# One copy moved ahead on ScalarE's list: the pad of the second chunk's keys

## The chip, the cores and the metric

The kernel runs on one core of a Trainium2 chip. The metric is the device time of one execution in microseconds (us). Five engines run their own instruction lists side by side and wait for each other by semaphores: TensorE (PE, matrix products into PSUM), VectorE (DVE), ScalarE (ACT), GpSimd (POOL) and SyncE (SP, which here only starts DMAs).

## What is computed

The input x has 2048 rows of 640 columns, in bf16. Its rows are normalised, and two branches are added to x:

```python
xn = _layernorm(x, axis=-1)
return x + _A_ref(xn, A_wqkv, A_wo) + _B_ref(xn, B_w1, B_b1, B_w2, B_b2)
```

Branch A is attention with 32 heads of 20 columns. Row s looks at 8 rows only, s, s-2, ..., s-14, so the keys and values of a row reach at most 14 rows back. Scores before row 0 are masked. Branch B is a two-layer perceptron, 640 to 1536 to 640, with gelu between.

## The kernel before

**Tiles.** The 2048 rows are cut into four chunks of 512 (the names use n = 0 to 3), each chunk into four blocks of 128 (j = 0 to 3). Activations stand transposed, features on the partitions and rows along the free dimension, in 5 tiles of 128 features. For each chunk `qT`, `kT` and `vT` hold queries, keys and values. `kT` and `vT` have 14 extra columns in front of each feature tile, the **pad**, which holds the last 14 rows of the chunk before, so that a window can reach back across the border.

**Stages of a chunk.** Mean and variance of the rows; normalised rows `xn` (line 262 on ScalarE), turned into `xnT` by a DMA on SP's queue (line 291, pieces `tc`); the projections q, k, v on TensorE (line 333, pieces `pj`, for the first chunk line 377, pieces `hj`), each copied from PSUM by ScalarE (line 397, pieces `pc`; line 392, pieces `hc`); the products q times k for the 8 window places on VectorE, one instruction per block (line 430, pieces `qk`); sums over feature tiles on VectorE (lines 465 and 471, pieces `pa`, `pb`) and over the columns of a head on TensorE (line 480, piece `lg`); the softmax (VectorE: maximum, difference, sum, lines 527 to 538; ScalarE: exponent, line 543, and reciprocal by Ln and Exp, lines 552 and 553, pieces `ri`); the weights spread over the partitions by DMAs (line 577, pieces `xe`); weights times values on VectorE (line 584, pieces `av`) and their sums. The perceptron runs beside this: line 614 (pieces `f1`) into PSUM, gelu on ScalarE (line 630, pieces `ge`), and line 696 (pieces `t`), which adds both branches up in PSUM.

**The order.** Nothing is scheduled by a program: the string `ORDER` names every piece of work once, the pieces are issued in that order, and each engine works through its own instructions in that order without overtaking. Waits come from the tiles: a reader waits for the writer, a writer waits for earlier readers of the same tile.

**PSUM banks.** The outputs of `pj`, `hj` and `f1` share one pool of four banks (`psA`). TensorE can begin such an output only when ScalarE has copied out one of those that hold the banks. ScalarE's place in its list therefore decides when TensorE goes on.

**Around the change.** The piece `pad11` is the pad of the keys (the second 1) of the second chunk (the first 1): one ScalarE copy of 5 times 14 columns per partition, line 404, out of the first chunk's keys into the second chunk's `kT`. The four products of the second chunk stand on VectorE in the order `qk11`, `qk13`, `qk12`, `qk10`. The products of blocks 1, 2 and 3 begin at column 128 or later of a feature tile, and only block 0 reads the pad columns. All four and the pad copy nevertheless touch the same tile, with the feature tiles of one between those of the other, and the built program orders them: a product that stands behind the pad copy in `ORDER` waits for it, and the pad copy waits for the products that stand ahead of it.

In `ORDER` of the kernel before, ScalarE has at this place: the last copies of the second chunk's q and k (the last one of k is `pc113`), a load of the activation table with exponents `ex0b` and `ex0a`, then `pc120`, `sq23`, `pc124`, `sq20` (squares for the third chunk's variance), `hc202`, `rs2` (lines 244 and 247), then `pad11`, `hc211`, `pc122`, `ri0b`, `ri0a`, `hc210`, a table load, `ge0_7`, `xn21`, `ge0_4`, `xn20`.

Of the kernel before, what the change touches and what calls it, by code (L numbers as in the profile page):

```python
# [43 lines left out]
xn10 hj012 hc110 tc10 hj011 pk xn11 hj111 hc012 tc11 hc010 qk00 hc011 hj112 hc111 f10_2 hc112 xn13 f10_0 xn12 tc13  # L44
qk02 f10_1 tc12 ge0_0 f10_5 ldx qk03 f10_11 ge0_5 f10_3 ge0_11 ge0_2 pj101 ge0_3 pa00 pj112 pc101 ge0_1 pj104 pc112
xp2 pa01 su20 pj110 xp0 pc104 ld2 su22 pj102 pc110 pb01 pj100 su21 hj201 su23 pc102 pb04 pj103 ng2 pc100 hc201 pj114
sq22 lg0 pc114 ldo pj111 cp0b cp0a sq21 mask pj113 m0b pc103 m0a pj124 pc111 mx0a pc113 mx0b t000 qk11 pj120 ex0b
hj202 ex0a hj210 pc120 sq23 ss0a hj211 pc124 ss0b sq20 pj122 qk13 hc202 rs2 f10_7 pad11 hc211 pc122 t040 ri0b f10_8
ri0a rc2 qk12 hc210 f10_4 f11_1 ge0_7 xn21 qk10 f11_3 ge0_4 tc21 xn20 pj121 ge1_3 tc20 t041 ge1_1 pa11 f11_9 ge0_8
xn23 hj212 pc121 tc23 t001 xn22 pa10 f10_6 hc212 tc22 ge1_9 f11_10 ge0_6 at0a at0b f10_9 ge1_10 pb11 xe01 su33 xe03  # L50
t002 xe00 ge0_9 pj123 pad21 su32 pb14 pj210 xe02 su31 pj203 xp1 pc210 su30 lg1 t042 pc203 av01 cp1b f10_10 ng3 f11_5
# [805 lines left out]
```

## Time and profile before

| what | value |
|---|---|
| median of 3 runs | 207.95 us (207.87 to 208.01) |
| the profiled execution | 207.52 us |
| its span, first to last instruction | 205.4 us |
| granted TensorE clock | 1.000 |
| busy: TensorE, VectorE, ScalarE, GpSimd | 200.2, 185.7, 129.0, 29.4 us |

The profile is of one execution. Times in its views are microseconds from the span's start. Each row of a timeline has the start, the length, the engine, the line in the kernel, what is written and read, and how many instructions are merged in the row; a bracket gives the idle time ahead of it and what ended that. Instructions of one engine can overlap by about a tenth of a microsecond in the records. TensorE's ends are modelled, so its starts are the better numbers.

### The profile page before, as it was taken

To read this page: it belongs to the slowest core of one execution; us is meant where nothing else is said; L and a number is where in the kernel's file an instruction comes from. 1 tells how busy PE (TensorE), PEld (TensorE's weight loads), DVE (VectorE), ACT (ScalarE), POOL (GpSimd) and SP (SyncE) were. 2 spreads that over 40 slices of the span, in tenths; PEclk is the share of its full clock that TensorE was granted. 3 is DMA by queue.
4 is the path that set the end of the run, shared out by engine and by line. 5 is a ranking of instruction groups with operands and counts; after the bars stand their busy time and mean duration, and the time that the engine had idled before them with its cause. 6 is when DMAs were issued, how large, how long until landed. Compare 5 with 4: busy or idle time off the path is not lost.

```text
span 205.4 us, 2870 instructions
## 1 busy us (share of the span) xinstructions
PE 200.2 (97%) x1100; PEld 105.1 (51%) x1100; DVE 185.7 (90%) x160; ACT 129.0 (63%) x237; POOL 29.4 (14%) x34
## 2 busy tenths in 40 slices
PE   8999999997899999999999999999999999999994
PEld 3998455573444555544445544444434454445552
DVE  2889998799995999999999998999979999998871
ACT  5679898887898799655284443996469942220100
POOL 2000000000000400022340040000022710253320
PEclk9999999999999999999999999999999999999999
DMA  6997499800428690759399181002845899893951
GB/s 207 391 396 191 104 378 337 305 0 0 67 64 218 178 191 4 199 117 142 79 161 121 19 97 15 3 0 39 191 51 93 146 102 161 134 107 57 101 89 64
DMA packets 38430, 27.31 MB, mean 133 GB/s; under 512 B 25106, under 2 KB 34578, under 8 KB 38418
## 3 DMA queue, kind: packets, MB, share of 16 engines
q1 hardware_dynamic: 28016, 20.39, 35.5%
q0 software_dynamic: 10080, 6.56, 28.0%
q10 hardware_dynamic: 322, 0.20, 0.3%
q8 instruction: 8, 0.13, 0.3%
q14 instruction: 4, 0.03, 0.0%
HBM read 10.49 MB, written 4.59 MB: 73 GB/s over the span
## 4 chain that ended last, share of the span: by engine, by line
PE 90%; DVE 5%; ACT 3%; issue 0%
PE T L696 26%; PE hps L614 23%; PE pps L333 21%; PE lo L652 5%; PE gps L377 5%; DVE prod L430 3%; PE idle L443 2%; PE both L652 2%; PE gps L346 1%; PE hi L652 1%; PE L L480 1%; DVE ax L529 1%; PE tp L279 1%; ACT L170 1%; ACT hT L630 1%; DVE ax L527 1%
## 5 line engine op out<-in xcount | busy, mean ns | idle before, releaser
L614 PE MATMUL hps<-xnT,w_sb 128*128 128x512 bf16 x240 | 56.3, 379 | 1.5 <-ACT vT L392 1.0
L430 DVE TENSOR_TENSOR prod<-qT,kT 128x5120 bf16<-128x5120 bf16 x16 | 44.6, 2821 | 1.4 <-ACT qT L397 1.0
L696 PE MATMUL T<-hT,w_sb 128*128 128x512 bf16 x180 | 44.6, 379 | 0.0
L614 PEld LDWEIGHTS <-w_sb 128*128 128x128 bf16 x240 | 23.4, 98 | 29.8 <-issue 2.3
L708 POOL DMA_DIRECT2D out_dram<-x_sb x15 | 20.8, 1593 | 67.1 <-DMA x_sb<-x_sb 67.1
L630 ACT ACTIVATE hT<-hps,bT 128x512 bf16<-128x512 f32 x36 | 23.8, 691 | 9.5 <-PE hps L614 9.1
L696 PEld LDWEIGHTS <-w_sb 128*128 128x128 bf16 x180 | 17.2, 98 | 20.9 <-issue 1.3
L584 DVE TENSOR_TENSOR prod<-vT,ax 128x5120 bf16<-128x5120 bf16 x8 | 22.4, 2821 | 3.6 <-PE L L480 3.6
L699 ACT ACTIVATE x_sb<-T,bT 128x512 bf16<-128x512 f32 x15 | 10.4, 693 | 21.6 <-PE T L696 19.2
L584 DVE TENSOR_TENSOR prod<-vT,x_sb 128x5120 bf16<-128x5120 bf16 x8 | 22.3, 2819 | 0.1
L595 POOL DMA_DIRECT2D prod<-prod x6 | 7.3, 1208 | 100.2 <-DVE prod L584 100.2
L170 ACT ACT_TABLE_LOAD x14 | 18.0, 1283 | 1.0 <-PEq L841 0.7
L471 DVE TENSOR_TENSOR prod<-prod 128x4096 bf16<-128x4096 bf16 x8 | 18.3, 2291 | 0.2
L333 PE MATMUL pps<-xnT,wv_sb 128*128 128x512 bf16 x75 | 18.3, 379 | 0.2
L696 PE MATMUL T<-oT,wo 128*128 128x512 bf16 x75 | 18.5, 379 | 0.0
L333 PE MATMUL pps<-xnT,wq_sb 128*128 128x512 bf16 x75 | 18.5, 379 | 0.0
L333 PE MATMUL pps<-xnT,wk_sb 128*128 128x512 bf16 x75 | 18.3, 379 | 0.0
L465 DVE TENSOR_TENSOR prod<-prod 128x4096 bf16<-128x4096 bf16 x8 | 18.1, 2287 | 0.1
L597 DVE TENSOR_TENSOR prod<-prod 128x2560 bf16<-128x2560 bf16 x10 | 14.6, 1484 | 0.0
L397 ACT CAST qT<-pps 128x512 bf16<-128x512 f32 x15 | 8.6, 583 | 7.2 <-PE pps L333 7.2
L333 PEld LDWEIGHTS <-wv_sb 128*128 128x128 bf16 x75 | 8.7, 117 | 7.8 <-issue 0.6
L333 PEld LDWEIGHTS <-wk_sb 128*128 128x128 bf16 x75 | 8.7, 118 | 7.7 <-issue 0.4
(96 smaller groups left out, 240.7 us busy)
## 6 DMA issues: line engine op xcount, KB each, us to landing
prod<-prod POOLq DMA_DIRECT2D x6, 640.0 KB, 6.5
ax<-attn SPq DMA_DIRECT2D x8, 256.0 KB, 4.3
x_sb<-attn SPq DMA_DIRECT2D x8, 256.0 KB, 4.2
w_sb<-in_B_w_dram SPq DMA_DIRECT2D x2, 960.0 KB, 11.5
out_dram<-x_sb SPq DMA_DIRECT2D x3, 640.0 KB, 5.0
w_sb<-in_B_w_dram SPq DMA_DIRECT2D x4, 480.0 KB, 6.9
out_dram<-x_sb POOLq DMA_DIRECT2D x15, 128.0 KB, 4.5
x_sb<-in_A_x_dram SPq DMA_DIRECT2D x2, 640.0 KB, 6.8
```

Of the source, the lines that this page charges most:

```text
L170: nc.scalar.preload_act_table_set(name)
L333: nc.tensor.matmul(ps[:], lhsT=wqkv_p[which][:, ti, to, :], rhs=xnT[:, ti, :], start=(ti == 0), stop=(ti == KT - 1),)
L430: nc.vector.tensor_tensor(out=prod[:, j], in0=q[:, :, at].unsqueeze(1).to_broadcast([P, W, KT, P]), in1=window(k, at), op=ALU.mult,)
L465: nc.vector.tensor_tensor(out=low, in0=low, in1=high, op=ALU.add)
L471: nc.vector.tensor_tensor(out=first, in0=first, in1=rows[:, :, t * P : (t + 1) * P], op=ALU.add)
L584: nc.vector.tensor_tensor(out=prod[:, j], in0=window(qkv_tile(n, 2), slice(j * P, (j + 1) * P)), in1=ax_view(n)[:, j, :, :].unsqueeze(2).t ...
L597: nc.vector.tensor_tensor(out=low, in0=low, in1=high, op=ALU.add)
L614: nc.tensor.matmul(ps[:], lhsT=w1_sb[:, ti, ft * P : (ft + 1) * P], rhs=tiles["xnT", n][:, ti, :], start=(ti == 0), stop=(ti == KT - 1),)
L630: nc.scalar.activation(hT, tiles["hps", n, ft][:], ACT.Gelu_apprx_tanh, bias=bT[:, ft : ft + 1], scale=1.0)
L652: nc.tensor.matmul(out_ps(bl, hi), lhsT=lhs, rhs=rhs[:, CH:D] if hi else rhs[:, 0:CH], start=pc == 0 and k == 0, stop=pc == 4 and k == len ...
L696: nc.tensor.matmul(ps[:], lhsT=lhs, rhs=rhs, start=pc == 0 and k == 0, stop=pc == 4 and k == len(srcs) - 1)
L708: nc.gpsimd.dma_start(dst, src, accum_op=ALU.add)
```

## The change

`pad11` is named 18 pieces earlier in `ORDER`: ahead of `qk11`, where it stood behind `qk13`, `rs2` and `f10_7`. No instruction is added or taken away, and no other piece changes its place against another.

```diff
-...mx0b t000 qk11 pj120 ex0b
-hj202 ex0a hj210 pc120 sq23 ss0a hj211 pc124 ss0b sq20 pj122 qk13 hc202 rs2 f10_7 pad11 hc211 pc122 t040 ri0b f10_8
+...mx0b t000 pad11 qk11 pj120
+ex0b hj202 ex0a hj210 pc120 sq23 ss0a hj211 pc124 ss0b sq20 pj122 qk13 hc202 rs2 f10_7 hc211 pc122 t040 ri0b f10_8
```

(The dots stand for the unchanged head of the first line.) On ScalarE the copy comes to stand between `pc113` and the table load. In the built program its single wait names `pc113`, the last write of `kT` ahead of it, where it named `qk13` before. `qk11` waits for the pad copy, where it waited for `pc113`. `qk12` has no wait left. The first Ln of `ri0b` (line 552) has a wait of its own for the last sum of `ss0b`, which the pad's wait covered before. The lists of the other engines are unchanged.

More of the change, by code (lines that the diff above doesn't have):

```diff
@@ L46 @@
 xp2 pa01 su20 pj110 xp0 pc104 ld2 su22 pj102 pc110 pb01 pj100 su21 hj201 su23 pc102 pb04 pj103 ng2 pc100 hc201 pj114
-sq22 lg0 pc114 ldo pj111 cp0b cp0a sq21 mask pj113 m0b pc103 m0a pj124 pc111 mx0a pc113 mx0b t000 qk11 pj120 ex0b
-hj202 ex0a hj210 pc120 sq23 ss0a hj211 pc124 ss0b sq20 pj122 qk13 hc202 rs2 f10_7 pad11 hc211 pc122 t040 ri0b f10_8
+sq22 lg0 pc114 ldo pj111 cp0b cp0a sq21 mask pj113 m0b pc103 m0a pj124 pc111 mx0a pc113 mx0b t000 pad11 qk11 pj120
+ex0b hj202 ex0a hj210 pc120 sq23 ss0a hj211 pc124 ss0b sq20 pj122 qk13 hc202 rs2 f10_7 hc211 pc122 t040 ri0b f10_8
 ri0a rc2 qk12 hc210 f10_4 f11_1 ge0_7 xn21 qk10 f11_3 ge0_4 tc21 xn20 pj121 ge1_3 tc20 t041 ge1_1 pa11 f11_9 ge0_8
```

## The prediction

> **What bounds the kernel now.** I read the page's first part, then busy time by stretches, the waits, and the rows of three engines from 39 to 65 us, where the moved copy stands.
>
> ```profile
> PE 200.2 (97%) x1100; PEld 105.1 (51%) x1100; DVE 185.7 (90%) x160; ACT 129.0 (63%) x237; POOL 29.4 (14%) x34
> ...
> 40.00:47.00 7.00, 6.96 (x44) 4.67 (x43) 6.86 (x8) 5.49 (x12) 0.00 (x0) 1.00 0.02 6
> 47.00:54.00 7.00, 5.37 (x25) 2.37 (x24) 6.75 (x5) 6.62 (x14) 0.00 (x0) 1.00 0.01 2
> 54.00:65.00 11.00, 11.00 (x60) 5.34 (x58) 8.69 (x6) 10.01 (x21) 0.00 (x0) 1.00 0.60 120
> 65.00:205.00 140.00, 137.64 (x701) 66.58 (x697) 130.18 (x91) 74.76 (x124) 27.90 (x22) 1.00 0.64 101
> ```
>
> The stretches give length, then busy time of PE, PEld, DVE, ACT and POOL, granted clock, DMA share, GB/s. TensorE is the bound: busy for all but 5.2 of 205.4 us. But 1.63 of those 5.2 lie between 47 and 54 us. Who is waited for there, in the waits between 36 and 66 us:
>
> ```profile
> DVE prod L584 <- PE L L480: 2.5, 1, 2.5
> ...
> ACT kT L404 <- DVE prod L430: 1.8, 1, 1.8
> PE hps L614 <- ACT vT L392: 1.0, 1, 1.0
> ...
> PE hps L614 <- ACT hT L630: 0.4, 1, 0.4
> ```
>
> Line 404 is the moved copy: it waits 1.8 us for a VectorE product, and TensorE then waits for copies that stand behind it on ScalarE. ScalarE's rows show the whole chain:
>
> ```profile
> 38.70 1.08 ACT L397 CAST kT<-pps 128x512 bf16<-128x512 f32 x2
> 39.80 1.28 ACT L170 ACT_TABLE_LOAD   x1
> 41.10 1.15 ACT L543 ACTIVATE e<-e 128x512 bf16<-128x512 bf16 x2
> 42.15 0.57 ACT L397 CAST vT<-pps 128x512 bf16<-128x512 f32 x1
> ...
> 45.32 0.21 ACT L247 ACTIVATE rstd<-logv 128x4 f32<-128x4 f32 x1
> 47.28 0.25 ACT L404 COPY kT<-kT 128x70 bf16<-128x70 bf16 x1 [1.75 <-DVE prod L430]
> 47.44 0.58 ACT L392 CAST vT<-gps 128x512 bf16<-128x512 f32 x1
> 47.92 0.59 ACT L397 CAST vT<-pps 128x512 bf16<-128x512 f32 x1
> 48.39 0.27 ACT L552 ACTIVATE ax<-ax 128x64 f32<-128x64 f32 x1
> 48.69 0.26 ACT L553 ACTIVATE rs<-ax 128x64 bf16<-128x64 f32 x1
> 48.86 0.24 ACT L552 ACTIVATE ax<-ax 128x64 f32<-128x64 f32 x1
> ...
> 51.17 0.69 ACT L630 ACTIVATE hT<-hps,bT 128x512 bf16<-128x512 f32 x1
> 51.76 0.91 ACT L262 ACTIVATE xn<-x_sb,nmr,rstd 128x640 bf16<-128x640 bf16 x1
> 52.57 0.68 ACT L630 ACTIVATE hT<-hps,bT 128x512 bf16<-128x512 f32 x1
> ```
>
> And TensorE's:
>
> ```profile
> 41.08 2.94 PE L377 MATMUL gps<-xnT,wv_sb 128*128 128x256 bf16 x25
> 44.07 1.24 PE L333 MATMUL pps<-xnT,wv_sb 128*128 128x512 bf16 x5
> 45.15 1.24 PE L614 MATMUL hps<-xnT,w_sb 128*128 128x512 bf16 x5
> 46.22 0.81 PE L696 MATMUL T<-hT,w_sb 128*128 128x512 bf16 x3
> 48.07 3.40 PE L614 MATMUL hps<-xnT,w_sb 128*128 128x512 bf16 x15 [1.03 <-ACT vT L392]
> 51.91 1.24 PE L614 MATMUL hps<-xnT,w_sb 128*128 128x512 bf16 x5 [0.44 <-ACT hT L630]
> 53.30 1.24 PE L333 MATMUL pps<-xnT,wv_sb 128*128 128x512 bf16 x5
> 54.37 0.81 PE L696 MATMUL T<-hT,w_sb 128*128 128x512 bf16 x3
> ...
> 64.51 0.61 PE L480 MATMUL L<-prod,head_of 128*32 128x512 bf16 x8
> ```
>
> Three starts follow ScalarE's ends by 0.04 to 0.05 us: 48.07 after line 392 (47.44 + 0.58 = 48.02), 51.91 after line 630 (51.17 + 0.69 = 51.86), 53.30 after line 630 (52.57 + 0.68 = 53.25). Each time a PSUM bank was missing. Undisturbed, five such products start 1.08 us apart (44.07 to 45.15) and three 0.65 apart, so from 46.22 the next starts would have been 46.87, then 3.24 us later, then 1.08 later: 51.19 for the group that started at 53.30. TensorE lost 2.11 us here, more than the idle figures say, because those use modelled ends. From 53.30 to 64.51 it runs without a gap.
>
> **The change part by part.** *What goes:* ScalarE is free at 45.32 + 0.21 = 45.53 and sits until 47.28. Behind it stand `hc211` and `pc122`, whose TensorE work ended before 45.4 by the rows at 41.08 and 44.07, and `ri0b`, whose sums VectorE ended before 44.5 (below). None of them needs `qk13`.
>
> *What is added:* one copy, after `pc113` (38.70 + 1.08 = 39.78). It waits for that copy's own end; the two waiting instructions of ScalarE above show the step, 48.39 + 0.27 = 48.66 to 48.69, 0.03 us. So it runs from 39.81 to 40.06, and the table load, which starts 0.02 after the copy ahead of it now, starts at 40.08: **0.28 us late**. Nothing absorbs this: ScalarE has no gap until 45.53, and the exponents already wait for the table, not for VectorE. The bounds of this cost come from a copy of the same size elsewhere:
>
> ```profile
> 62.13 0.27 ACT L406 COPY kT<-kT 128x70 bf16<-128x70 bf16 x1
> 62.27 0.77 ACT L225 ACTIVATE trash<-x_sb 128x640 bf16<-128x640 bf16 x1
> ```
>
> It holds up its successor by 0.14 only, because neighbours overlap. From below that is the bound, since a copy that is executed is not free; from above I take twice my value, 0.56. I take 0.28, because here both neighbours forbid the overlap. [...]
>
> *ScalarE after the move:* line 247 ends at 45.81. A follower with no wait starts 0.09 ahead of the end of the one before (48.69 + 0.26 = 48.95 against 48.86), so `hc211` starts at 45.72 instead of 47.44. **ScalarE is 1.72 us earlier** from there, with the same instructions up to `ge0_4`, which ends at 51.53.
>
> *TensorE after the move:* the starts at 44.07, 45.15 and 46.22 are paced by banks that ScalarE empties between 42.7 and 45.1, so they slip by 0.28. From 46.50 it goes on undisturbed: 47.15 (its bank is free at 46.30), 50.39 (`ge0_7` ended at 50.14), and then the group that started at 53.30 could start at 51.47, but waits for `ge0_4` until 51.58. **1.72 us earlier**, and so is everything to line 480: 64.51 becomes 62.79. On the way `xn21` starts at 50.04, its turning by SP's DMA with it, and SP's later entries, which stand in a row behind that, by as much; the DMAs are idle there (share 0.02 and 0.01 from 40 to 54 us), so nothing is in the way.
>
> *VectorE:* here a wait is added, of `qk11` for the copy.
>
> ```profile
> 39.17 0.76 DVE L538 TENSOR_TENSOR e<-e,ax 128x512 bf16<-128x512 bf16 x2
> 39.85 2.82 DVE L430 TENSOR_TENSOR prod<-qT,kT 128x5120 bf16<-128x5120 bf16 x1
> ...
> 43.96 0.55 DVE L529 TENSOR_TENSOR ax<-ax 128x128 f32<-128x128 f32 x2
> 44.43 2.82 DVE L430 TENSOR_TENSOR prod<-qT,kT 128x5120 bf16<-128x5120 bf16 x1
> 47.17 0.15 DVE L252 TENSOR_TENSOR nmr<-neg,rstd 128x4 f32<-128x4 f32 x1
> 47.56 5.56 DVE L430 TENSOR_TENSOR prod<-qT,kT 128x5120 bf16<-128x5120 bf16 x2 [0.24 <-ACT kT L404]
> ...
> 58.12 4.61 DVE L471 TENSOR_TENSOR prod<-prod 128x4096 bf16<-128x4096 bf16 x2
> 65.22 5.56 DVE L584 TENSOR_TENSOR prod<-vT,ax 128x5120 bf16<-128x5120 bf16 x2 [2.49 <-PE L L480]
> ```
>
> `qk11` starts at 40.09 instead of 39.85, 0.24 late, and all of VectorE queues behind it. The exponents end at 42.25 + 0.28 = 42.53, before the sums need them at 42.83. `qk13` ends at 47.49, line 252 runs from 47.41, and the third product, now without a wait, starts at 47.53 (0.12 after line 252's start, which is that instruction's length less the usual overlap) instead of 47.56. The 0.24 is given back there. VectorE reaches the end of line 471 at 62.70 instead of 62.73, and line 480 needs it. Before, VectorE was ready 1.78 us ahead of TensorE; after, 62.70 + 0.05 = 62.75 against 62.79: **the two arrive together**. This is what is late next, and it leaves no cover: each further tenth that `qk11` loses costs a tenth at the end.
>
> *After that:* line 584 waits for line 480, so VectorE restarts 1.72 earlier too. Its other condition is the spread weights, whose DMA stands on SP behind the turned rows:
>
> ```profile
> 57.70 2.52 SPq L291 DMA_TRANSPOSE xnT<-xn  x2
> 60.31 0.67 SPq L577 DMA_DIRECT2D ax<-attn  x1
> ...
> DMA to landing us min/median/max: 3.8/4.4/5.2
> ```
>
> The last row is of the four issues of line 577. At 4.4 us the first lands at 64.7 now, 63.0 after; VectorE can restart at 63.4 (line 480 takes 0.55 to the next start). From here all engines keep their distances, and TensorE is busy for 137.64 of the last 140 us.
>
> *Sum:* 0.28 lost at 40, 2.00 won at 47 (1.75 of wait and 0.25 of copy), -1.72 us. The profiled execution took 207.52 (span 205.4 and 2.1 around it) and would take 205.8. The median of the runs is 207.95, 0.43 above it, so I forecast **206.2 us**.
>
> **The rivals.** *VectorE becomes the bound.* If the copy costs its upper bound, `qk11` starts 0.52 late, the product chain ends at 63.0, and the gain is 1.4: 206.5. A late landing of the spread weights (5.2 instead of 4.4 us) would hold VectorE's restart until 63.8, 0.4 late, though VectorE has waits of its own behind it to take that up. Together the gain would be between 0.5 and 1.3: 206.7 to 207.4. For it speaks that the slack of 1.78 is used up; against it that every term has its row.
>
> *Nothing changes.* ScalarE is busy for 63% only and TensorE for 97%; gaps on ScalarE would then be free and the time stays at 207.9. [...] The stretch from 47 to 54 us, with 5.37 of 7.00 busy, speaks against it. It would hold only if TensorE's three late starts had another cause or were given back later.
>
> *The copy is held up at its new place.* This ends on the slower side. `qk11`, the table load, the exponents and all copies queue behind it, VectorE without a gap to line 480. The chain has 1.78 + 0.27 = 2.05 us to give (the slack, and the 0.27 won at `qk12`); beyond that the end moves out. If the copy had to wait as long as one VectorE product takes (2.82, and 0.25 for itself), line 480 would come 1.0 later and the time would be 209.0. Against it: its only wait is for a ScalarE copy that ends at 39.78.
>
> *The change does not do what it says:* excluded, as the built lists show the copy at its new place and the wait of `qk12` gone.
>
> **How the numbers follow.** Forecast (gain of 1.3 to 2.0, 205.9 to 206.6): 0.68. VectorE the bound: 0.18. Nothing changes: 0.07. Held up: 0.07. The range from 205.9 to 207.4 holds the first two, 0.86. Faster by over 0.2% (0.4 us, about what a measurement here can tell from no change): 0.68 + 0.18 = 0.86; within: 0.07; slower: 0.07.
>
> **What would show it.** Right: the copy at 39.8 with no wait of note, `qk11` at 40.1, no idle ScalarE ahead of line 392 at 45.7, TensorE's group of 53.30 at 51.6, VectorE's 2.49 us of idle ahead of line 584 shrunk to about 0.7, all later rows 1.7 earlier. Wrong: a gap ahead of line 480 that ends with line 471, a wait at the copy, or a gap that opens after 63 us.

## The result, and the profile after

| | before | after |
|---|---|---|
| median | 207.96 us (13 runs, 207.68 to 212.51) | 206.07 us (13 runs, 205.85 to 208.36) |
| profiled execution, its span | 207.52, 205.4 | 205.97, 203.8 |
| ratio after to before | | 0.9915, 95% interval 0.9892 to 0.9938 |

The change makes the kernel 0.85% faster, 1.77 us by the ratio. The forecast was 206.2. Ratios leave out runs that were disturbed, so a median below can stand above what its ratio gives (pad_late_filled).

The two profiles don't start alike: a later part of x landed later in the one of after (VectorE's statistics, line 213, wait 0.19 for it until 10.66, where they start at 10.47 without a wait before), and line 480 of the first chunk starts at 35.73 instead of 35.53. So 0.20 is taken off the times of after wherever they are compared with those of before, and the **distance from line 480's start in the first chunk to its start in the second** serves as the measure for all kernels below: it spans the place of the change and leaves the varying start out. It was 64.51 - 35.53 = 28.98 us and is 62.96 - 35.73 = 27.23: 1.75 less. From there to the end both profiles take the same, 140.9 and 140.8 us.

The page's busy times and the two stretches by time, of after:

```profile
PE 199.9 (98%) x1100; PEld 105.1 (52%) x1100; DVE 185.8 (91%) x160; ACT 128.9 (63%) x237; POOL 29.3 (14%) x34
```

```profile
40.00:47.00 7.00, 6.79 (x44) 4.66 (x43) 6.70 (x9) 6.93 (x16) 0.00 (x0) 1.00 0.06 21
47.00:54.00 7.00, 7.00 (x34) 3.23 (x33) 7.00 (x5) 6.91 (x13) 0.00 (x0) 1.00 0.15 34
```

From 47 to 54 us TensorE is busy for 7.00 of 7.00 us, where it was 5.37. From 40 to 47 it lost a little, 6.79 against 6.96. ScalarE's rows of after show why:

```profile
38.89 1.08 ACT L397 CAST kT<-pps 128x512 bf16<-128x512 f32 x2
40.01 0.25 ACT L404 COPY kT<-kT 128x70 bf16<-128x70 bf16 x1
40.27 1.28 ACT L170 ACT_TABLE_LOAD   x1
...
45.79 0.20 ACT L247 ACTIVATE rstd<-logv 128x4 f32<-128x4 f32 x1
45.91 0.57 ACT L392 CAST vT<-gps 128x512 bf16<-128x512 f32 x1
...
49.63 0.69 ACT L630 ACTIVATE hT<-hps,bT 128x512 bf16<-128x512 f32 x1
50.21 0.91 ACT L262 ACTIVATE xn<-x_sb,nmr,rstd 128x640 bf16<-128x640 bf16 x1
51.02 0.68 ACT L630 ACTIVATE hT<-hps,bT 128x512 bf16<-128x512 f32 x1
```

The copy has no idle time ahead of it any more, and line 392 follows line 247 at once, where 1.75 us of waiting and the copy stood between them. TensorE's rows and VectorE's, of after:

```profile
41.27 1.80 PE L377 MATMUL gps<-xnT,wv_sb 128*128 128x256 bf16 x15
43.24 1.25 PE L377 MATMUL gps<-xnT,wv_sb 128*128 128x256 bf16 x10 [0.17 <-ACT vT L397]
44.53 1.24 PE L333 MATMUL pps<-xnT,wv_sb 128*128 128x512 bf16 x5
...
47.34 4.48 PE L614 MATMUL hps<-xnT,w_sb 128*128 128x512 bf16 x20
51.75 1.24 PE L333 MATMUL pps<-xnT,wv_sb 128*128 128x512 bf16 x5
...
62.96 0.62 PE L480 MATMUL L<-prod,head_of 128*32 128x512 bf16 x8
```

```profile
40.29 2.83 DVE L430 TENSOR_TENSOR prod<-qT,kT 128x5120 bf16<-128x5120 bf16 x1 [0.17 <-ACT kT L404]
...
47.61 0.15 DVE L252 TENSOR_TENSOR nmr<-neg,rstd 128x4 f32<-128x4 f32 x1
47.68 5.55 DVE L430 TENSOR_TENSOR prod<-qT,kT 128x5120 bf16<-128x5120 bf16 x2
...
58.22 4.61 DVE L471 TENSOR_TENSOR prod<-prod 128x4096 bf16<-128x4096 bf16 x2
63.67 2.83 DVE L584 TENSOR_TENSOR prod<-vT,ax 128x5120 bf16<-128x5120 bf16 x1 [0.83 <-ACT trash L225]
```

The groups that started at 48.07 and 51.91 (line 614) and 53.30 (line 333) run from 47.34 on with no gap that the rows show. ScalarE still sets the start of the last one by a little: 51.75 is 0.05 behind `ge0_4`'s end (51.02 + 0.68 = 51.70), and 20 products at 1.08 for five would have let it start at 51.66. What the change costs is seen too: 0.17 of idle time at 43.24, and VectorE's 0.17 ahead of the first product. VectorE's idle time ahead of line 584 fell from 2.49 to 0.83 us (about 0.7 was forecast). The row names ScalarE's line 225 as what ended it, but the instruction waits for no such result: in the built program its waits are for line 471, line 480, the spread weights and a line 392 that ended at 48.3. It starts 0.09 after the last product of line 480 (63.58 in the chain), as before (65.13, then 65.22). In pad_mid and pad_dve below the same wait is put down to line 480. A releaser is inferred from what ended last.

### The profile page after: what moved, and what is told of

Read it like the earlier page. It is cut to its first block, busy times and chain, and to the rows that moved or that the text cites. A ratio compares the mean times of both kernels' runs of the same rounds, so it can differ in the third digit from the quotient of the medians.

```text
span 203.8 us, 2870 instructions
## 1 busy us (share of the span) xinstructions
PE 199.9 (98%) x1100; PEld 105.1 (52%) x1100; DVE 185.8 (91%) x160; ACT 128.9 (63%) x237; POOL 29.3 (14%) x34
## 4 chain that ended last, share of the span: by engine, by line
PE 84%; ACT 7%; DMA 4%; DVE 2%; SPq 1%; issue 1%
PE T L696 27%; PE hps L614 23%; PE pps L333 22%; PE lo L652 5%; DMA x_sb<-in_A_x_dram 4%; PE both L652 2%; DVE stats L213 2%; ACT xn L262 2%; PE gps L377 1%; PE hi L652 1%; ACT L170 1%; PE L L480 1%; ACT qT L392 1%; ACT e L543 1%; ACT kT L392 1%
```

## The experiments

The theory under test, called the queue theory: the gain is the end of ScalarE's wait for `qk13` and of the bank shortage behind it. Its main rival, the VectorE theory: the gain comes from the products, the third of which no longer waits for the copy. The others: gaps on an engine busy for 63% cost nothing; the place ahead of the table load is good in itself. All kernels at a glance; the starts of line 480 are those of the profiles:

| kernel | line 480, first and second chunk | distance against before | median, us | ratio to before, interval |
|---|---|---|---|---|
| before | 35.53, 64.51 | | 207.96 | |
| after | 35.73, 62.96 | -1.75 | 206.07 | 0.9915, 0.9892 to 0.9938 |
| after_again | 35.58, 62.81 | -1.75 | 206.20 | 0.9927, 0.9896 to 0.9958 |
| pad_mid | 36.81, 63.98 | -1.81 | 206.09 | 0.9908, 0.9880 to 0.9936 |
| pad_dve | 35.84, 63.01 | -1.81 | 206.24 | 0.9906, 0.9882 to 0.9931 |
| pad_late | 35.85, 68.41 | +3.58 | 211.34 | 1.0147, 1.0111 to 1.0183 |
| pad_held | 37.19, 68.66 | +2.49 | 211.18 | 1.0128, 1.0069 to 1.0187 |
| before_extra | 35.81, 64.80 | +0.01 | 207.90 | 0.9984, 0.9962 to 1.0007 |
| after_extra | 36.04, 64.47 | -0.55 | 207.31 | 0.9972, 0.9959 to 0.9985 |
| pad_late_filled | 38.15, 69.92 | +2.79 | 211.50 | 1.0138, 1.0103 to 1.0173 |
| pad_held_filled | 35.62, 65.72 | +1.12 | 209.09 | 1.0067, 1.0040 to 1.0094 |

**after_again**, the changed kernel as a yardstick.

> The changed kernel once more, as the yardstick of this group. Queue theory (the gain is the end of ScalarE's wait for qk13, and TensorE's three late starts behind it): 206.2 us, 1.7 below the kernel before, the copy at 40.0, line 392 following line 247 without a gap, line 480 at 62.8 to 63.0. Nothing else is expected to move.

As expected, to the hundredth in the distance.

**pad_mid**, another place on ScalarE without the wait (the lines are those of after and of pad_mid, cut at the dots):

```diff
- ... t000 pad11 qk11 pj120 ex0b hj202 ex0a hj210 pc120 sq23 ss0a ...
+ ... t000 qk11 pj120 ex0b hj202 ex0a hj210 pc120 pad11 sq23 ss0a ...
```

> The copy stands behind qk11 in the list and behind pc120 on ScalarE. Queue theory: it waits for qk11, which ends at 42.67, just as ScalarE comes to it (42.7), so for about nothing; qk11 and the table load are not late any more (0.24 and 0.28 in the changed kernel), and ScalarE loses some 0.2 at 42.9 instead. Line 392 then starts 1.79 earlier than before, and the time is 206.1, the same as the changed kernel within 0.1. VectorE theory (the gain came from the products, which start and end earlier, and VectorE sets line 480): VectorE is ready 0.27 earlier than in the changed kernel and the time falls by as much, to 205.9.

ScalarE's rows of pad_mid:

```profile
43.42 0.57 ACT L397 CAST vT<-pps 128x512 bf16<-128x512 f32 x1
43.97 0.25 ACT L404 COPY kT<-kT 128x70 bf16<-128x70 bf16 x1
44.12 0.82 ACT L232 ACTIVATE trash<-x_sb,neg 128x640 bf16<-128x640 bf16 x1
```

And VectorE's (1.28 is to be taken off):

```profile
59.04 4.61 DVE L471 TENSOR_TENSOR prod<-prod 128x4096 bf16<-128x4096 bf16 x2
64.69 2.83 DVE L584 TENSOR_TENSOR prod<-vT,ax 128x5120 bf16<-128x5120 bf16 x1 [1.04 <-PE L L480]
```

The copy sits between two others with no idle time, though it waits for `qk11`: that product had just ended. VectorE was ready at 63.65 - 1.28 = 62.37, 0.26 earlier than in after, yet the distance fell by 0.06 only, not by 0.27. So VectorE doesn't set line 480 here. The place ahead of the table load is not what matters either: this second place, also without a wait, does as well.

**pad_dve**, the copy at its old place in the list, on another engine (against before):

```diff
-            nc.scalar.copy(dest[:, :, 0:PAD], pair_of(1, 1)[:, :, 2 * P :])
+            nc.vector.tensor_copy(dest[:, :, 0:PAD], pair_of(1, 1)[:, :, 2 * P :])
```

> The copy at its old place in the list, but on VectorE, between qk13 and line 252; ScalarE has one copy less. Queue theory: ScalarE goes from line 247 straight on to line 392, 2.0 earlier than before (45.4); on VectorE the copy takes 0.1 to 0.2 and the third product starts near 47.5 as before, so VectorE is ready for line 480 at 62.7 and sets it: 1.75 gained, 206.2. VectorE theory: the third product starts no earlier than before, so nothing is gained, 207.9.

VectorE's and then TensorE's rows of pad_dve (0.31 is to be taken off):

```profile
47.58 0.18 DVE L404 COPY kT<-kT 128x70 bf16<-128x70 bf16 x1
47.68 0.15 DVE L252 TENSOR_TENSOR nmr<-neg,rstd 128x4 f32<-128x4 f32 x1
47.80 5.57 DVE L430 TENSOR_TENSOR prod<-qT,kT 128x5120 bf16<-128x5120 bf16 x2
```

```profile
63.01 0.62 PE L480 MATMUL L<-prod,head_of 128*32 128x512 bf16 x8 [0.16 <-DVE prod L471]
```

The third product starts at 47.49, against 47.56 before: VectorE gained 0.07, and the kernel 1.81. The **VectorE theory falls** here: the gain is there without an earlier VectorE, as soon as ScalarE doesn't wait. And TensorE now waits 0.16 for line 471 at line 480: ScalarE, freed even of the copy, lets TensorE arrive first, and VectorE sets the end of the stretch, as expected.

**pad_late**, the old place with a longer wait (against before, cut at the dots):

```diff
- ... f10_7 pad11 hc211 pc122 t040 ri0b f10_8 ri0a rc2 qk12 hc210 ...
+ ... f10_7 rc2 qk12 pad11 hc211 pc122 t040 ri0b f10_8 ri0a hc210 ...
```

> ScalarE's order as in the kernel before; line 252 and qk12 are named ahead of the copy, so that the copy waits for one product more (its only new wait), and the third product waits for nothing. Queue theory: the copy runs at 50.0 instead of 47.28, line 392 starts 2.74 later, all three late starts of TensorE grow, line 480 comes at 67.25 and the time is 210.7. VectorE theory: VectorE is 0.3 earlier, so the time is unchanged or 0.3 lower, 207.7 to 207.9. Theory that gaps on an engine busy for 63% cost nothing: 207.9.

ScalarE's rows, TensorE's, and the stretches behind the gap, of pad_late (0.32 is to be taken off):

```profile
50.41 0.25 ACT L404 COPY kT<-kT 128x70 bf16<-128x70 bf16 x1 [4.56 <-DVE prod L430]
50.56 0.58 ACT L392 CAST vT<-gps 128x512 bf16<-128x512 f32 x1
```

```profile
51.19 6.16 PE L614 MATMUL hps<-xnT,w_sb 128*128 128x512 bf16 x20 [3.85 <-ACT vT L392]
57.19 1.24 PE L333 MATMUL pps<-xnT,wv_sb 128*128 128x512 bf16 x5
```

```profile
46.00:51.00 5.00, 1.35 (x7) 0.49 (x5) 4.69 (x4) 0.59 (x2) 0.00 (x0) 1.00 0.00 0
51.00:53.00 2.00, 1.81 (x5) 0.66 (x5) 2.00 (x1) 1.92 (x8) 0.00 (x0) 0.61 0.00 0
53.00:55.00 2.00, 2.00 (x6) 0.74 (x5) 2.00 (x2) 1.99 (x3) 0.00 (x0) 0.54 0.00 0
55.00:57.00 2.00, 2.00 (x11) 0.91 (x10) 2.00 (x2) 2.00 (x3) 0.00 (x0) 1.00 0.00 0
```

The wait grew by one product, from 1.75 to 4.56, and the time rose: a longer wait costs more, and both rivals (no change, or less) fall. On ScalarE everything is as forecast (line 392 at 50.56 less 0.32 is 50.24, 2.80 later than before). But the distance grew by 3.58 instead of 2.74. The stretches show what was not in the forecast: after 3.85 us without work TensorE's granted clock is 0.61 and 0.54 in the next two stretches of 2 us, and 20 products of line 614 take 6.16 us, where they take 4.48 in after. From 55 to 57 it is 1.00 again.

**pad_held**, the copy held up at its new place, which the prediction had as the rival on the slower side (against after):

```diff
- ... t000 pad11 qk11 pj120 ...
+ ... t000 qk11 pad11 pj120 ...
```

> The copy ahead of the table load on ScalarE as in the changed kernel, but named behind qk11, so that it waits for qk11 to end (42.7). This is the case of the copy held up at its new place. Queue theory: ScalarE stands from 39.8 to 42.7, the exponents end at 45.4 instead of 42.3, VectorE's sums and qk13 come 2.8 later and VectorE is ready for line 480 at about 65.3; TensorE, held by the banks, comes to it at 65.7 instead of 64.5, so 1.15 is lost: 209.1. A theory by which the place ahead of the table load is good in itself: below 207.9.

ScalarE's and TensorE's rows of pad_held, and two stretches behind the gap (1.66 is to be taken off):

```profile
44.34 0.25 ACT L404 COPY kT<-kT 128x70 bf16<-128x70 bf16 x1 [2.91 <-DVE prod L430]
...
50.12 0.21 ACT L247 ACTIVATE rstd<-logv 128x4 f32<-128x4 f32 x1
50.23 0.57 ACT L392 CAST vT<-gps 128x512 bf16<-128x512 f32 x1
51.60 0.59 ACT L397 CAST vT<-pps 128x512 bf16<-128x512 f32 x1 [0.80 <-PE pps L333]
```

```profile
47.56 2.29 PE L377 MATMUL gps<-xnT,wv_sb 128*128 128x256 bf16 x10 [3.03 <-ACT vT L397]
49.65 1.91 PE L333 MATMUL pps<-xnT,wv_sb 128*128 128x512 bf16 x5
```

```profile
47.50:49.50 2.00, 1.94 (x10) 1.35 (x10) 1.87 (x6) 2.00 (x6) 0.00 (x0) 0.52 0.00 0
49.50:51.50 2.00, 2.00 (x8) 0.86 (x7) 2.00 (x1) 1.27 (x6) 0.00 (x0) 0.63 0.00 0
```

The same place on ScalarE as in after, with a wait, and the kernel is 1.3% slower than before: it is the wait, not the place. Line 392 came where it was forecast (50.23 - 1.66 = 48.57, 1.13 later than before). Again the size was off, 211.2 for 209.1, and again TensorE had a gap, of 3.03 us, and worked slowly behind it, at a granted clock of 0.52 and 0.63: 2.29 us for the ten products that take 1.25 in after. One of the four runs had the full clock on average (1.000 instead of 0.992), and that run took 209.0 us.

**before_extra and after_extra**, the slack of VectorE at line 480, by an instruction whose result nothing reads:

```diff
+    spare = consts.tile([P, 2560], BF16, name="spare")
+    def do_dm():
+        half = w1_sb[:].rearrange("p t f -> p (t f)")
+        nc.vector.tensor_tensor(out=spare[:], in0=half[:, 0:2560], in1=half[:, 2560:5120], op=ALU.add)
- ... pad21 su32 pb14 pj210 ...
+ ... pad21 su32 dm pb14 pj210 ...
```

> The kernel before with one VectorE instruction added that nothing reads (an addition of 2560 columns, 1.48 us alone, 1.41 in a row), ahead of the last line 471 of the second chunk. VectorE was ready 1.78 ahead of line 480, so it is now ready at 64.1 and line 480 still starts at 64.5. Queue theory: no change, 207.9. Theory that VectorE, busy for 90%, is the bound: 1.4 more, 209.4.

> The changed kernel with the same added VectorE instruction at the same place. Queue theory: VectorE and TensorE arrive together at line 480 in the changed kernel, so the 1.41 is paid: line 480 comes 1.3 to 1.4 later, 207.5. Theory that the changed kernel still has VectorE slack there: 206.1.

TensorE's row of each, first before_extra, then after_extra, and VectorE's of after_extra (the added lines move line 480 to 486; 0.51 is to be taken off in after_extra):

```profile
64.80 0.62 PE L486 MATMUL L<-prod,head_of 128*32 128x512 bf16 x8
```

```profile
64.47 0.62 PE L486 MATMUL L<-prod,head_of 128*32 128x512 bf16 x8 [1.13 <-DVE prod L471]
```

```profile
60.74 1.48 DVE L477 TENSOR_TENSOR spare<-w_sb 128x2560 bf16<-128x2560 bf16 x1
62.14 2.28 DVE L471 TENSOR_TENSOR prod<-prod 128x4096 bf16<-128x4096 bf16 x1
```

The same instruction costs nothing in the kernel before (+0.01 in the distance, 0.9984 in time) and 1.20 in the changed one, a little less than the 1.3 to 1.4 expected. It delayed the end of line 471 by 1.28 there and not by 1.41 (64.42 - 0.51 = 63.91 against 62.63), because the two instructions of line 471 stand 0.05 apart when they are alone; of the 1.28, 0.08 was still hidden. This is the forecast's "the two arrive together", measured.

**pad_late_filled and pad_held_filled**, the clock alone. Products of constants, which nothing reads, fill TensorE's gap (16 as shown, 14 in pad_held_filled; the last two lines are against pad_late on the left and pad_held on the right):

```diff
+    def do_fl():
+        spare = psL.tile([P, W, P], F32, tag="L", name="fill")
+        for _ in range(16):
+            nc.tensor.matmul(spare[:].rearrange("p w c -> p (w c)")[:, 0:CH],
+                             lhsT=ones[:, 0:P], rhs=ones[:], start=True, stop=True)
- ... t040 ri0b f10_8 ...        - ... hj210 pc120 ...
+ ... t040 fl ri0b f10_8 ...     + ... hj210 fl pc120 ...
```

> pad_late with 16 products of constants that nothing reads (3.5 us) put into the gap in which TensorE waits there, ahead of the group of line 614 that waits. Clock theory (pad_late took 0.6 more than forecast because the granted clock fell to 0.54 to 0.61 for some 4 us after a gap of 3.85 us): no gap, the clock stays at 1.00, the 20 products of line 614 take 4.5 instead of 6.2, line 480 starts 2.8 later than in the kernel before (3.6 in pad_late), and the time is 210.7 although TensorE does more work. Theory that the rest of pad_late's loss is more waiting for ScalarE: 211.3 as in pad_late.

> pad_held with 14 such products (3.0 us) in its gap, between the two groups of line 377. Clock theory: the clock stays at 1.00, line 480 starts 1.15 later than in the kernel before (2.5 in pad_held's profile), and the time is 209.1, the value forecast for pad_held, which one of its four runs showed (209.0, at clock 1.000). Theory that the copy's place ahead of the table load costs more than the wait: 211.2 as in pad_held.

TensorE's rows and a stretch behind the filled gap, first pad_late_filled, then pad_held_filled (2.62 and 0.09 are to be taken off):

```profile
49.48 3.66 PE L454 MATMUL fill<-const-bfloat16-1.0 128*128 128x512 bf16 x16
53.49 3.40 PE L625 MATMUL hps<-xnT,w_sb 128*128 128x512 bf16 x15 [0.35 <-ACT vT L392]
57.32 1.24 PE L625 MATMUL hps<-xnT,w_sb 128*128 128x512 bf16 x5 [0.44 <-ACT hT L641]
...
53.00:55.00 2.00, 1.65 (x9) 0.68 (x8) 2.00 (x1) 1.94 (x7) 0.00 (x0) 1.00 0.04 8
```

```profile
42.80 3.22 PE L454 MATMUL fill<-const-bfloat16-1.0 128*128 128x512 bf16 x14
46.00 1.25 PE L377 MATMUL gps<-xnT,wv_sb 128*128 128x256 bf16 x10
47.29 1.24 PE L333 MATMUL pps<-xnT,wv_sb 128*128 128x512 bf16 x5
...
46.00:48.00 2.00, 1.96 (x15) 1.51 (x14) 1.90 (x6) 2.00 (x6) 0.00 (x0) 1.00 0.00 0
```

With more work for TensorE the distance shrank, to +2.79 (forecast 2.8) and +1.12 (1.15), and pad_held_filled took 209.09 us, the forecast of pad_held. Ten products of line 377 took 1.25 again. The work behind the gap starts at the same time with and without the filling (line 614 at 51.19 - 0.32 = 50.87 and 53.49 - 2.62 = 50.87; line 377 at 47.56 - 1.66 = 45.90 and 46.00 - 0.09 = 45.91), so only what follows differs: within 0.05 us the clock was the rest of both misses. The time of pad_late_filled is the less sharp number: its ratio gives 210.8, with 210.1 to 211.5 by the interval, which holds both 210.7 and 211.3. The distance decides there. It comes from an execution with a mean clock of 0.992 and a late start (38.15); in every stretch from 35 to 70 us, and so over the distance up to its end at 69.92, the clock was 1.00.

No kernel beats the changed one by more than these runs can tell; pad_mid and pad_dve are ahead by 0.06 us in the distance.

## Why the prediction was right

Point by point, the times of after less 0.20:

- *The copy's own cost, 0.28 on ScalarE.* It ran from 39.81 (39.81 forecast) and the table load began at 40.07 (40.08). The forecast took the copy without an overlap, and the trace shows none at this place: the copy starts 0.04 after the end of the one it waits for (38.89 + 1.08 = 39.97, then 40.01), and the table load 0.01 after the copy's (40.01 + 0.25 = 40.26, then 40.27). Between neighbours without a wait there is one, such as 0.08 between lines 247 and 392 (45.79 + 0.20 = 45.99 against 45.91).
- *ScalarE 1.72 earlier.* Line 392 at 45.71 (45.72), `ge0_4` ended at 51.50 (51.53).
- *TensorE.* Line 333's group at 44.33, 0.26 later than before (0.28); the group of 53.30 at 51.55 (51.58); line 480 at 62.76 (62.79).
- *VectorE.* `qk11` at 40.09 (40.09), third product at 47.48 (47.53), ready at 62.63 (62.70). It was 0.07 better than forecast; 0.05 of that is that line 252 held up its follower by 0.07, not 0.12. after_extra showed the slack left, 0.08.
- *Nothing given back later.* 140.8 us from line 480 to the end, 140.9 before.
- *The sum.* 1.72 forecast, 1.75 in the distance, 1.77 by the ratio.

The rivals: VectorE as the bound was near, but came true only where ScalarE was freed further (pad_dve, 0.16 of wait) or VectorE loaded (after_extra). "Nothing changes" was refuted by the result itself, and by pad_late, where a longer gap on the little used ScalarE cost 1.5%. TensorE, the busiest engine, was the one to look at; what held it up stood on ScalarE. For the copy held up, the prediction gave 1.0 us, 209.0 in all, reckoned through VectorE's chain, which had 2.05 us to give. With the clock kept up the number holds (209.09), but in part by luck: in pad_held_filled VectorE is ready 0.39 ahead of line 480 (60.71 + 4.62 = 65.33 against 65.72), and TensorE, held up for want of a bank at line 377 (it starts at 46.00, behind line 397's end at 45.38 + 0.56 = 45.94), sets it. Without the filling the price was 3.3 us in the median. There the prediction failed in size: it left TensorE's own gap out of this rival, and the clock behind the gap with it.

## What to carry to other kernels

A cheap instruction that waits at the head of an engine's queue holds up what stands behind it, and costs time where the busiest engine needs that (here a copy of 0.25 us waited for 1.75, and the distance was 1.75 longer than without the wait): look for the wait that ends last on the busy engine, then go back through the queue of the engine that it names. A copy that must keep out of the way of readers of the same tile did equally well ahead of the first of them and just behind its end (-1.75 us in after, -1.81 in pad_mid). Before moving it, find the slack of the other chain at their next meeting point (1.78 us here), since the gain cannot be larger than that slack and what is won beside it.

## What the runs showed of the hardware

TensorE's granted clock was lower behind the long gaps in its work. In the kernel before, a gap of 1.03 us (by the modelled ends) left it at 1.00 in the stretch from 47 to 54 us. After 3.03 us it fell in pad_held's profile, and three of four runs had a lower mean clock (0.992, the fourth 1.000); after 3.85 us it fell in pad_late's, and in four runs of four (0.992). In pad_held it is 0.52 from 47.5 to 49.5, 0.63 from 49.5 to 51.5 and 1.00 from 51.5 to 60; in pad_late it is 0.61 from 51 to 53, 0.54 from 53 to 55 and 1.00 from 55 to 70. What the clock lacks of 1.00 in these 4 us makes the same loss in both, an estimate from the four averages: (0.48 + 0.37) x 2 = 1.70 us and (0.39 + 0.46) x 2 = 1.70 us. The rows of line 614 in pad_late agree, 6.16 - 4.48 = 1.68 for its 20 products. Products of constants in the gap kept the clock at 1.00, from 46 to 70 us in pad_late_filled and from 42 to 60 in pad_held_filled.

Nor do these runs give a length below which a gap is harmless: no kernel was built to leave a gap between 1.03 and 3.03 us.

The time ahead of line 480's first start varied from 35.53 to 37.19 us between profiles whose instructions up to there are the same, and was 38.15 in pad_late_filled's. That is about as much as the effect that was studied, so a distance between two rows inside the trace told the kernels apart better than whole times.
